# Weights behind the last v, one load for the gate, and ranks between two halves of the scores in a fused attention and top-1 expert kernel

## The chip, the cores and the metric

One core of a Trainium2 chip runs the whole kernel. The metric is the device time of one execution in microseconds (us), lower is better; the kernel before took 479.04 us (median of three runs, 478.44 to 480.1).

## The reference

Lightning attention (batch 4, 8 heads, 768 positions, head size 64, blocks of 64 with a decaying key-value state) gives a 3072 x 512 matrix `x`. Each row goes to the one expert of eight with the highest gate logit:

```python
logits = x @ w_gate                       # 512 x 8
expert_idx = np.argmax(logits, axis=1)
gate_w = softmax(logits)[row, expert_idx]
for e in range(8):
    xe = x[expert_idx == e]
    out[expert_idx == e] = gate_w * (np.maximum(xe @ w1[e], 0) @ w2[e])   # 512x1024, 1024x512
```

## The kernel before

**Attention.** The work is cut into six steps `n` of 128 positions and, in each, two pairs of batches `b` = 0 and 2; I write (n,b) for such a piece, and twelve of them follow each other. For one piece `enter` starts the loads of q, k and v of (n+1,b) on SP's queue (512 KB each, three buffers), turns q and k on TensorE (`turn_q`, `turn_k`, L207) and copies them on ScalarE. `score` (L242) makes the scores in two halves of heads `s`, and VectorE masks them with the decay into `mt` (L248, four per piece). `attend_states` (L267), `grow` (L293, `cp`) and `attend` (L276) give the output `op` and the new state. The main loop overlaps three pieces: it leaves the last one (`leave`, `rows`: TensorE turns the output back and multiplies by the gate in one go with `back`, tile `tx`, L320; ScalarE copies it and stores it to `xs` in device memory, L329), enters the next, and attends the current one.

**Routing.** When the four batches of a step have left, `choose` finds the expert of each row on VectorE (`oh`, one-hot) and adds the one-hots up batch by batch (`ohc`, L364). `put` (L375) then multiplies on TensorE: `before` (strictly upper triangular) by `oh`, and `ones` by the sums `ohc`; that is each row's rank among the rows of its expert. VectorE adds the expert's base and makes the address `slot_i` (L384 to L389), and GpSimd scatters the entries to `slots` in device memory (L391, two per piece). The first four steps fill the list of expert 0 early: when the entries of step 3 are stored, `start_early` loads `list_0a` on SP's queue (L416), gathers its 256 rows `xg` (L440) and runs them through expert 0 as pass 0a while the last rows of attention finish.

**Experts.** Passes 0a, 0b and experts 1 to 7 follow. `ph`, `po` and `p` are TensorE's matrix products there.

**What sets the order.** Instructions that are pinned (`pin`) keep the program's order on their engine; the others are placed by a scheduler. A wait on one of an engine's instructions holds all behind it. Loads that SP and ScalarE issue take completion semaphores in turn, and a load waits for the one that last used its semaphore. On-chip accumulators are eight banks: scores 0 to 3, `cp` 4, `rank` 5, `op` 6 and 7, `tx` 4 to 7. The last `tx` on banks 6 and 7 has to be copied out before the next `op` goes there.

Of the kernel before, what the change touches and what calls it, by code (L numbers as in the profile page):

```python
# [10 lines left out]
F32 = mybir.dt.float32  # L11
BF16 = mybir.dt.bfloat16
I32 = mybir.dt.int32
AX = mybir.AxisListType
# [7 lines left out]
def kernel(  # L22
# [29 lines left out]
    nc = tc.nc  # L52
    B, H, S, D = q.shape
# [112 lines left out]
    def pick(per_e, e):  # L166

        if isinstance(e, int):
            return per_e[e]
        return per_e[bass.ds(e, 1)].squeeze(0)  # L170

    def load_weights(e):
        w1t = wpool.tile([P, DC, F], F32, tag="w1", name="w1t")
        nc.sync.dma_start(out=w1t, in_=pick(w1_r, e))
        w2t = wpool.tile([P, FC, MD], F32, tag="w2", name="w2t")
        nc.sync.dma_start(out=w2t, in_=pick(w2_r, e))
        return w1t, w2t

    weights = []
# [9 lines left out]
    def bank(i, shape, name):  # L189
        return ps.tile(shape, F32, tag=f"bank{i}", name=name)  # L190
# [7 lines left out]
    def pin(inst):  # L198
        tc.keep_in_program_order(inst)
# [109 lines left out]
                    out=sd, in0=to, in1=sdec.unsqueeze(1).to_broadcast(shp), op=ALU.mult))  # L309
                nc.vector.tensor_add(to, m.cp, sd)  # L310

    def rows(m, b, lg):

        x = work.tile([P, MD], F32, tag="x", name="x", bufs=3)
        tx = [bank(4 + 2 * b + w, [P, HP // 2, 2, W], f"tx{w}") for w in range(2)]
        for hp in range(HP):
            c, j = hp // 2, hp % 2
            for w, t in ((0, 0), (1, 1), (0, 1), (1, 0)):
                flat = tx[w].rearrange("p c j w -> p c (j w)")
                pin(nc.tensor.matmul(  # L320
                    flat[halves[t], c, j * D:j * D + W],
                    lhsT=m.xT[b][halves[w], hp, halves[t]], rhs=back[halves[w], b, hp, :],
                    start=(hp == 0), stop=(hp == HP - 1), skip_group_check=True))
        to = x.rearrange("p (c j u e) -> p u c j e", c=HP // 2, j=2, u=2)
        for w, t in enumerate(tx):
            nc.scalar.copy(lg[:, w], t[:, :, 0, D:])
            nc.scalar.copy(to[:, w ^ b], t[:, :, :, :D])  # L327
        r0 = 1 + (m.n * B + m.b + b) * C
        nc.scalar.dma_start(out=xs[r0:r0 + C, :], in_=x)  # L329

    def choose(n, bs, lg):
        nb = len(bs)
        shp = [P, nb, E]
        parts, lg = lg, small.tile(shp, F32, tag="lg_sum", name="lg_sum")
        pin(nc.vector.reduce_sum(lg, parts.rearrange("p b w c e -> p b e (w c)"), axis=AX.X))
        mx = small.tile([P, nb, 1], F32, tag="mx", name="mx")
# [12 lines left out]

        more = 1 if (n, bs) == early else 0  # L350
        oh = small.tile([P, nb + more, E], BF16, tag=f"oh{more}", name="oh")
        if more:
            nc.gpsimd.memset(oh[:, nb], 0.0)
        nc.vector.tensor_tensor(out=oh[:, :nb], in0=key, in1=pick.to_broadcast(shp), op=ALU.is_equal)

        sm = small.tile([P, nb], F32, tag="sm", name="sm")
        nc.vector.reduce_sum(sm, ex, axis=AX.X)
        nc.vector.tensor_scalar_add(sm, sm, 1e-9)
        nc.vector.reciprocal(entry[:, n, bs[0]:bs[0] + nb, 2], sm)

        ohc = small.tile([P, nb + 1, E], BF16, tag="ohc", name="ohc")
        nc.vector.tensor_copy(ohc[:, 0], so_far[0])
        for i in range(nb):
            nc.vector.tensor_add(ohc[:, i + 1], ohc[:, i], oh[:, i])  # L364
        so_far[0] = ohc[:, nb]
        return n, bs, oh, ohc

    def put(n, bs, oh, ohc):


        nb = len(bs)
        shp = list(oh.shape)
        rank = bank(5, shp, "rank")
        for lhs, rhs in ((before, oh), (ones, ohc[:, :shp[1]])):
            mm = nc.tensor.matmul(rank, lhsT=lhs, rhs=rhs, start=(lhs is before),  # L375
                                  stop=(lhs is ones))

            if (n, bs[-1]) != (NSTEP - 1, B - 1):
                pin(mm)
        if shp[1] > nb:  # L380
            nc.vector.tensor_copy(had, rank[:, nb, 0:1])
        shp[1] = nb
        place = small.tile(shp, F32, tag="place", name="place")
        nc.vector.tensor_add(place, rank[:, :nb], base[0].unsqueeze(1).to_broadcast(shp))  # L384
        nc.vector.tensor_mul(place, place, oh[:, :nb])
        slot = small.tile([P, nb], F32, tag="slot", name="slot")
        nc.vector.reduce_sum(slot, place, axis=AX.X)
        slot_i = small.tile([P, nb], I32, tag="slot_i", name="slot_i")
        nc.vector.tensor_copy(slot_i, slot)  # L389
        def store(i):  # L390
            put = nc.gpsimd.indirect_dma_start(  # L391
                out=slots, out_offset=bass.IndirectOffsetOnAxis(ap=slot_i[:, i:i + 1], axis=0),
                in_=entry[:, n, bs[i], :], in_offset=None)

            tc.declare_no_dep(put.ins, group="put", reason="disjoint rows of the lists")
            tc.add_to_no_dep_group("put", put.ins)
            return put

        return store
# [254 lines left out]
    def enter(n, b):  # L654
        if n + 1 < NSTEP:
            loaded[n + 1, b] = load(n + 1, b)
        if (n, b) == (NSTEP - 2, B - 2):
            weights.append(load_weights(0))
        m = SimpleNamespace(n=n, b=b, qT=[], qsT=[], kT=[], kd=[], mt=[], xT=[])
        m.q, m.k, m.v = loaded[n, b]  # L660

        for s, turn_one in (((0, turn_q), (1, turn_q), (0, turn_k), (1, turn_k)) if not (n or b)
                            else ((0, turn_q), (0, turn_k), (1, turn_q), (1, turn_k))):
            turn_one(m, s)
        return m
# [19 lines left out]
    def give_places(group):  # L685

        waiting.append((group, put(*group), 0))

    def leave(m):
        for b in range(2):  # L690
            n, bs = group_of[m.n, m.b + b]
            i = bs.index(m.b + b)
            if i == 0:
                lgs[0] = small.tile([P, len(bs), 2, HP // 2, E], F32, tag="lg", name="lg")
            rows(m, b, lgs[0][:, i])
            if i == len(bs) - 1:

                pending.append((n, bs, lgs[0]))
# [25 lines left out]
    for s in range(2):  # L724
        score(cur, s)

    by_chunk = moe_w_gate.rearrange("(c j u d) e -> j u d c e", c=HP // 2, j=2, u=2)
    for j, u, b in itertools.product(range(2), range(2), range(2)):
        pin(nc.scalar.dma_start(
            out=back[halves[u ^ b], b, j::2, D - j * D:D - j * D + E], in_=by_chunk[j, u]))  # L730
    for i in range(len(order)):
        if last:
            leave(last)

        ahead = enter(*order[i + 1]) if 0 < i < len(order) - 1 else None
        attend_begin(cur)
        if cur.n < NSTEP - 1:
            attend_states(cur)
            decide()
# [12 lines left out]
        if i == 0:  # L752
            ahead = enter(*order[1])
        update(cur)
        if i == 0:
            later_decays()

        if chosen:
            give_places(chosen.pop())
        if ahead:  # L760
            store_places()
        if i == 1:
            empty_lists()
        if ahead and cur.n < NSTEP - 1:
            for s in range(2):
                score(ahead, s)
        last, cur = cur, ahead
    leave(last)
    decide()
    store_places(lambda inst: inst)  # L770
    give_places(chosen.pop())
    store_places(lambda inst: inst)


# [122 lines left out]
```

## Time and profile before

| | |
|---|---|
| median of three runs | 479.04 us |
| the profiled execution: its time, its span | 477.91 us, 476.1 us |
| TensorE matmul busy | 443.6 us (93%) |
| TensorE weight load busy | 367.0 us (77%) |
| VectorE, ScalarE, GpSimd busy | 243.7, 130.8, 252.9 us |
| moved by DMA | 72.71 MB, mean 153 GB/s |

The span is from the first to the last instruction; 1.8 us of the execution lie around it. Times in the rows are from the span's start. PE is TensorE's matmuls, PEld its weight loads, DVE VectorE, ACT ScalarE, POOL GpSimd, SP the engine that issues most loads; a q behind the name is the sequencer or queue of that engine. In brackets stands how long an engine was idle before an instruction and what ended the idle time. [...] TensorE's busy time is modelled, so a busy TensorE is not one at its peak.

### The profile page before, as it was taken

The page shows a single profiled execution, that of the slowest core. Times are in us where ns is not written, and L with a number is a line of the kernel's source. Part 1 is how long each engine was busy: PE and PEld are TensorE (multiplying, and loading weights), DVE is VectorE, ACT ScalarE, POOL GpSimd, SP SyncE. Part 2 cuts the span into 40 slices and gives each one's busy share as a digit, 9 for nine tenths or more (in the row PEclk, how much of TensorE's full clock was granted, in tenths as well). Part 3 has the DMA queues.
Part 4 walks back from the last instruction along what each step waited for, and adds up shares of the span by engine and source line. Part 5 has one row for each costly group of instructions (what it writes and reads, how often), then busy time and mean ns, then how long its engine had stood idle before and what let it go on. Part 6 is the DMA issues. An engine that isn't in the chain of part 4 may idle for free.

```text
span 476.1 us, 9780 instructions
## 1 busy us (share of the span) xinstructions
PE 443.6 (93%) x4023; PEld 367.0 (77%) x4023; DVE 243.7 (51%) x481; ACT 130.8 (27%) x327; POOL 252.9 (53%) x204
## 2 busy tenths in 40 slices
PE   4778988879789999999999999999999999999994
PEld 4667887869668484984996699599689779879863
DVE  3637475566634018475248534934843753564421
ACT  3334644443531022230123212212312311311210
POOL 6124445544243889985927663883793764531001
PEclk9979999999989999999999999999999999999998
DMA  9999999999723946735235360624426316001001
GB/s 178 177 233 256 240 207 236 222 296 260 171 87 97 375 121 201 245 100 173 86 136 176 91 220 1 234 79 174 178 83 222 124 73 222 1 18 46 1 19 51
DMA packets 100422, 72.71 MB, mean 153 GB/s; under 512 B 81811, under 2 KB 81815, under 8 KB 100368
## 3 DMA queue, kind: packets, MB, share of 16 engines
q1 hardware_dynamic: 90608, 52.49, 42.3%
q0 software_dynamic: 5008, 13.16, 8.7%
q10 hardware_dynamic: 4752, 6.33, 4.0%
q8 instruction: 34, 0.56, 0.5%
q14 instruction: 20, 0.16, 0.1%
HBM read 58.90 MB, written 13.16 MB: 151 GB/s over the span
## 4 chain that ended last, share of the span: by engine, by line
PE 70%; issue 3%; DMA 1%; POOL 1%; DVE 1%; POOLq 0%; ACT 0%
PE p L553 27%; PE p L581 18%; PE po L612 17%; PE ph L477 4%; PE tp L463 3%; DMA xg<-xs,list_0a 1%; POOL slots L391 0%; PE op L267 0%; PE tx L320 0%; POOLq L850 0%; DVE o L593 0%; PE rank L375 0%; DVE xgT L468 0%; POOL out_dram L446 0%; DVE hT L456 0%
## 5 line engine op out<-in xcount | busy, mean ns | idle before, releaser
L612 PE MATMUL po<-w2t,hT 128*128 128x512 f32 (+5 forms) x224 | 81.0, 596 | 0.0
L612 PEld LDWEIGHTS po<-w2t,hT 128*128 128x128 f32 (+5 forms) x224 | 30.5, 161 | 38.2 <-issue 37.9
L446 POOL DMA_INDIRECT out_dram<-o,list x24 | 23.7, 987 | 60.2 <-DVE o L618 31.6
L564 ACT ACTIVATE hT<-hT 128x408 f32<-128x408 f32 (+4 forms) x56 | 29.5, 527 | 90.5 <-DVE hT L562 90.5
L232 POOL TENSOR_TENSOR kd<-k_in,kdec 128x512 f32<-128x512 f32 x20 | 20.4, 1037 | 48.4 <-issue 22.2
L553 PE MATMUL p<-xgT,w1t 128*128 128x204 f32 (+4 forms) x224 | 41.5, 328 | 0.0
L553 PEld LDWEIGHTS p<-xgT,w1t 128*128 128x128 f32 x224 | 37.6, 190 | 1.2 <-issue 0.9
L517 POOL TENSOR_TENSOR t_q<-w2t 128x1024 f32<-128x1024 f32 x7 | 16.5, 2357 | 39.9 <-PE p L553 39.9
L391 POOL DMA_INDIRECT slots<-entry,slot_i x24 | 23.6, 981 | 23.2 <-DVE slot_i L389 15.5
L248 DVE TENSOR_TENSOR mt<-sp,decay 128x512 f32<-128x512 f32 x48 | 29.9, 682 | 10.5 <-PE sp L242 10.4
L593 DVE SCALAR_TENSOR_TENSOR o<-p,list,o 128x256 f32<-128x256 f32 x28 | 13.6, 484 | 32.9 <-PE p L581 17.0
L440 POOL DMA_INDIRECT xg<-xs,list x24 | 25.8, 1074 | 6.6 <-issue 5.0
L242 PEld LDWEIGHTS sp<-qT,kT 64*128 64x128 f32 x384 | 22.4, 188 | 7.4 <-ACT xT L285 4.2
L218 DVE TENSOR_TENSOR qsT<-tq,qdec 128x512 f32<-128x512 f32 x20 | 13.8, 692 | 26.3 <-ACT qT L214 26.3
L581 PE MATMUL p<-w2t,hT 128*128 128x256 f32 x112 | 26.8, 382 | 0.0
L581 PEld LDWEIGHTS p<-w2t,hT 128*128 128x128 f32 x112 | 21.0, 190 | 7.0 <-issue 4.5
L242 PE MATMUL sp<-qT,kT 64*128 64x128 f32 x384 | 24.8, 279 | 0.7 <-ACT kT L226 0.6
L517 POOL TENSOR_TENSOR t_v<-w2t 128x1024 f32<-128x1024 f32 x7 | 16.5, 2359 | 16.3 <-PE p L553 16.3
L276 PE MATMUL op<-mt,v_in 128*64 128x128 f32 x384 | 23.3, 273 | 1.2 <-ACT x L327 1.2
L207 PE MATMUL tq<-ident,q_in 128*128 128x128 f32 x96 | 16.9, 304 | 7.6 <-DMA q_in<-in_q_dram 7.6
L562 DVE TENSOR_TENSOR hT<-p,u_qsT 128x408 f32<-128x408 f32 (+4 forms) x28 | 15.7, 560 | 15.8 <-PE p L553 15.8
L477 PE MATMUL ph<-xgT,w1t 128*128 128x256 f32 (+1 forms) x128 | 23.0, 337 | 0.0
(159 smaller groups left out, 931.2 us busy)
## 6 DMA issues: line engine op xcount, KB each, us to landing
w1t<-in_moe_w_dram SPq DMA_DIRECT2D x8, 2048.0 KB, 7.9
w2t<-in_moe_w_dram SPq DMA_DIRECT2D x8, 2048.0 KB, 9.5
v_in<-in_v_dram SPq DMA_DIRECT2D x12, 512.0 KB, 8.7
xs<-x ACTq DMA_DIRECT2D x24, 256.0 KB, 5.9
q_in<-in_q_dram SPq DMA_DIRECT2D x11, 512.0 KB, 8.9
k_in<-in_k_dram SPq DMA_DIRECT2D x11, 512.0 KB, 8.3
q_in<-in_q_dram SPq DMA_DIRECT2D x2, 256.0 KB, 4.6
k_in<-in_k_dram SPq DMA_DIRECT2D x2, 256.0 KB, 5.3
```

The lines of the kernel that those rows point to most:

```text
L242: pin(nc.tensor.matmul(sp[u][:, i, b, :], lhsT=m.kT[s][halves[u], i, b, :], rhs=m.qT[s][halves[u], i, b, :], start=(i == 0 and b == 0), st ...
L248: nc.vector.tensor_mul(mt[:, u], sp[u], decay[:, u, s * HP // 2:(s + 1) * HP // 2].unsqueeze(2).to_broadcast(shp))
L276: pin(nc.tensor.matmul(out_at(m, b, u, hp), lhsT=m.v[:, b, 2 * hp + u, :], rhs=m.mt[hp // 2][:, u, hp % 2, b, :], start=(first and hp == 0 ...
L391: put = nc.gpsimd.indirect_dma_start(out=slots, out_offset=bass.IndirectOffsetOnAxis(ap=slot_i[:, i:i + 1], axis=0), in_=entry[:, n, bs[i] ...
L440: nc.gpsimd.indirect_dma_start(out=dst, out_offset=None, in_=xs[:rows, :], in_offset=bass.IndirectOffsetOnAxis(ap=idx, axis=0))
L446: put = nc.gpsimd.indirect_dma_start(out=out, out_offset=bass.IndirectOffsetOnAxis(ap=idx, axis=0), in_=src, in_offset=None, bounds_check= ...
L477: nc.tensor.matmul(ph, lhsT=w1t[:, dc, fc * P:(fc + 1) * P], rhs=m.xgT[:, dc, :], start=(dc == 0), stop=(dc == DC - 1))
L517: return nc.gpsimd.tensor_tensor(out=o, in0=x, in1=y, op=ALU.subtract)
L553: nc.tensor.matmul(p[:, i, :], lhsT=lhs[:, dc, (c + i) * P:(c + i + 1) * P], rhs=rhs[:, dc, :], start=(dc == 0), stop=(dc == DH - 1))
L564: nc.scalar.activation(outs[i][k], outs[i][k], ACT.Relu)
L581: nc.tensor.matmul(p, lhsT=lhs[:, fc, :], rhs=rhs[:, fc, :], start=(fc == 0), stop=(fc == FC // 2 - 1))
L612: nc.tensor.matmul(po[part], lhsT=m.hT[:, fc, t * P:t * P + w], rhs=w2t[:, fc, :], start=(i < k), stop=(i >= FC - k), skip_group_check=True)
```

## The change

The loads of expert 0's weights are pinned behind the load of the last v. The gate weights come in one load to a tile `gates`, from which GpSimd makes eight copies into `back`, in place of eight loads. The ranks of a step are made between the two halves of the scores; the sums over batches are made by TensorE (`ones` times the one-hots of the first i batches, added to the columns of the batches behind), and VectorE keeps only one running sum `so_far`. ScalarE copies the ranks out of the bank, and the first address operation is pinned behind the masks before it. The rows of the last piece but one use banks 2 and 3 in place of 6 and 7.

```diff
-    def load_weights(e):
+    def load_weights(e, pin=lambda inst: inst):
...
-        nc.sync.dma_start(out=w1t, in_=pick(w1_r, e))
+        pin(nc.sync.dma_start(out=w1t, in_=pick(w1_r, e)))
...
-        tx = [bank(4 + 2 * b + w, [P, HP // 2, 2, W], f"tx{w}") for w in range(2)]
+        tx = [bank(banks[b] + w, [P, HP // 2, 2, W], f"tx{w}") for w in range(2)]
...
+        new = small.tile([P, E], F32, tag="new", name="new")
+        nc.vector.reduce_sum(new, oh[:, :nb].rearrange("p b e -> p e b"), axis=AX.X)
+        old, so_far[0] = so_far[0], small.tile([P, E], BF16, tag="so_far", name="so_far", bufs=3)
+        nc.vector.tensor_add(so_far[0], old, new)
...
-        ohc = small.tile([P, nb + 1, E], BF16, tag="ohc", name="ohc")
-        nc.vector.tensor_copy(ohc[:, 0], so_far[0])
-        for i in range(nb):
-            nc.vector.tensor_add(ohc[:, i + 1], ohc[:, i], oh[:, i])
...
+    def ranks(n, bs, oh, old):
...
+        terms = [(rank, before, oh),
+                 (rank, ones, old.unsqueeze(1).to_broadcast(shp))]
+        terms += [(rank[:, all_b - i:], ones, oh[:, :i]) for i in range(last, 0, -1)]
...
+        got = small.tile(shp, F32, tag=f"rank{all_b - nb}", name="rank_in")
+        nc.scalar.copy(got, rank)
...
-            weights.append(load_weights(0))
+            weights.append(load_weights(0, pin))
...
-    for j, u, b in itertools.product(range(2), range(2), range(2)):
-        pin(nc.scalar.dma_start(
-            out=back[halves[u ^ b], b, j::2, D - j * D:D - j * D + E], in_=by_chunk[j, u]))
+    gates = const.tile([P, HP, E], F32, name="gates")
+    pin(nc.scalar.dma_start(out=gates, in_=moe_w_gate.rearrange("(c p) e -> p c e", p=P)))
+    for j, b, u in itertools.product(range(2), range(2), range(2)):
+        nc.gpsimd.tensor_copy(back[halves[u ^ b], b, j::2, D - j * D:D - j * D + E],
+                              gates[halves[u], j::2, :])
...
-            leave(last)
+            leave(last, (4, 6) if i < len(order) - 1 else (4, 2))
...
+        score_now = ahead and cur.n < NSTEP - 1
+        if score_now:
+            score(ahead, 0)
+        ranked = give_ranks()
+        if score_now:
+            score(ahead, 1)
+        for group in ranked:
+            give_places(group)
```

On SP's queue the loads of the last pieces stood in this order before (names with the number of their buffer: 1336 to 1338 are (4,2), 1548 to 1550 (5,0), 1725 to 1727 (5,2)):

```order
L93 DMA q_in_1548<-in_q_dram 128x16x64
L174 DMA w1t_1731<-in_moe_w1_dram 128x4x1024
L93 DMA v_in_1338<-in_v_dram 128x16x64
L93 DMA k_in_1549<-in_k_dram 128x16x64
L93 DMA q_in_1725<-in_q_dram 128x16x64
L93 DMA v_in_1550<-in_v_dram 128x16x64
L93 DMA k_in_1726<-in_k_dram 128x16x64
L176 DMA w2t_1733<-in_moe_w2_dram 128x8x512
L93 DMA v_in_1727<-in_v_dram 128x16x64
L416 DMA list_0a_2041<-slots_64 128x2x4
```

and now in this one (1344 to 1346 are (4,2), 1559 to 1561 (5,0), 1736 to 1738 (5,2)):

```order
L93 DMA q_in_1559<-in_q_dram 128x16x64
L93 DMA k_in_1560<-in_k_dram 128x16x64
L93 DMA v_in_1346<-in_v_dram 128x16x64
L93 DMA q_in_1736<-in_q_dram 128x16x64
L93 DMA k_in_1737<-in_k_dram 128x16x64
L93 DMA v_in_1561<-in_v_dram 128x16x64
L93 DMA v_in_1738<-in_v_dram 128x16x64
L174 DMA w1t_1742<-in_moe_w1_dram 128x4x1024
L176 DMA w2t_1744<-in_moe_w2_dram 128x8x512
L429 DMA list_0a_2082<-slots_64 128x2x4
```

Both weight loads have moved behind all loads of q, k and v, and both still stand ahead of `list_0a`.

On TensorE this stood at the first of four like places (steps 0 to 3), where `op` is the attention of one piece and `sp` the scores of the next, which go on for 14 more rows:

```order
L276 MATMUL op_601<-mt,v_in 64x128 x2
L375 LDWEIGHTS before
L375 MATMUL rank<-oh,before 128x32
L375 LDWEIGHTS ones
L375 MATMUL rank<-ohc,ones 128x32
L242 MATMUL sp_695<-qT,kT 128x128
L242 MATMUL sp_696<-qT,kT 128x128
```

and now, from the end of the first half of the scores (682, 683) to the second (703, 704):

```order
L242 MATMUL sp_683<-qT,kT 128x128
L378 LDWEIGHTS before
L378 MATMUL rank<-oh,before 128x32
L378 LDWEIGHTS ones
L378 MATMUL rank<-none_yet,ones 128x32
L378 LDWEIGHTS ones
L378 MATMUL rank<-oh,ones 128x24
L378 LDWEIGHTS ones
L378 MATMUL rank<-oh,ones 128x16
L378 LDWEIGHTS ones
L378 MATMUL rank<-oh,ones 128x8
L242 MATMUL sp_703<-qT,kT 128x128
```

Eight score matmuls now stand between the attention and the ranks, and the ranks are five matmuls, of which only `oh` is new from VectorE.

On VectorE, at the fourth place (step 3, whose entries fill `list_0a`), the addresses stood ahead of the masks:

```order
L362 COPY ohc<-ohc 128x8
L381 COPY had<-rank 128x1
L384 TENSOR_TENSOR place<-rank,ebase 128x32
L712 TENSOR_SCALAR skip<-had 128x1
L385 TENSOR_TENSOR place<-place,oh 128x32
L714 TENSOR_SCALAR skip<-skip 128x1
L387 TENSOR_REDUCE slot<-place 128x4
L717 TENSOR_TENSOR ebase_late<-ebase_late,skip 128x1
L389 CAST slot_i<-slot 128x4
L248 TENSOR_TENSOR mt<-sp_1868,decay 128x512
```

and now they stand among them:

```order
L248 TENSOR_TENSOR mt<-sp_1864,decay 128x512
L392 COPY had<-rank_in 128x1
L395 TENSOR_TENSOR place<-rank_in,ebase 128x32
L728 TENSOR_SCALAR skip<-had 128x1
L398 TENSOR_TENSOR place<-place,oh 128x32
L730 TENSOR_SCALAR skip<-skip 128x1
L400 TENSOR_REDUCE slot<-place 128x4
L733 TENSOR_TENSOR ebase_late<-ebase_late,skip 128x1
L248 TENSOR_TENSOR mt<-sp_1885,decay 128x512
L248 TENSOR_TENSOR mt<-sp_1886,decay 128x512
L402 CAST slot_i<-slot 128x4
```

The cast that GpSimd's scatter waits for has moved behind all four masks; ScalarE's copy `rank_in` lies between the ranks and `had`.

## Rows read from the trace of the kernel before

**Rows 1.** Chain that ended last: start us, us, what.

```profile
114.46 12.31 issue
...
128.86 5.53 DMA xg<-xs,list_0a
...
144.31 10.47 PE ph L477 x48
```

**Rows 2.** Seven stretches: busy time and instructions of each engine, PEclk, DMA share, GB/s.

```profile
10.00:14.00 4.00, 4.00 (x86) 3.88 (x88) 2.95 (x5) 0.39 (x1) 0.44 (x1) 1.00 1.40 216
14.00:18.00 4.00, 3.12 (x34) 2.50 (x32) 2.63 (x8) 2.40 (x6) 2.04 (x2) 1.00 0.48 75
23.00:30.00 7.00, 4.08 (x24) 3.41 (x26) 1.09 (x2) 1.92 (x4) 0.00 (x0) 0.51 1.07 237
30.00:115.00 85.00, 75.72 (x1716) 68.48 (x1714) 54.29 (x134) 38.53 (x117) 42.44 (x50) 1.00 1.09 239
115.00:125.00 10.00, 10.00 (x200) 9.29 (x198) 5.86 (x18) 4.91 (x15) 0.00 (x0) 1.00 1.11 308
135.00:139.00 4.00, 3.72 (x40) 2.90 (x41) 1.34 (x6) 1.67 (x4) 0.14 (x2) 0.58 0.01 1
145.00:469.00 324.00, 324.00 (x1614) 261.72 (x1612) 161.02 (x243) 70.07 (x147) 191.64 (x111) 1.00 0.38 128
```

**Rows 3.** Timeline from 7 to 28 us: start us, us, engine, line, what.

```profile
7.89 2.34 SPq L93 DMA_DIRECT2D k_in<-in_k_dram  x1
9.81 5.75 ACTq L729 DMA_DIRECT2D back<-in_moe_w_gate_dram  x8
15.70 0.37 SPq L93 DMA_DIRECT2D v_in<-in_v_dram  x1
23.13 1.09 PE L207 MATMUL tq<-ident,q_in 128*128 128x128 f32 x4 [2.12 <-DMA q_in<-in_q_dram]
27.00 1.09 PE L207 MATMUL tk<-ident,k_in 128*128 128x128 f32 x4 [2.79 <-DMA k_in<-in_k_dram]
```

**Rows 4.** Waits of SP's queue, whole run: who, whom for, us in total, times, longest.

```profile
SPq L416 <- DMA slots<-entry,slot_i: 8.7, 1, 8.7
SPq L93 <- DMA back<-in_moe_w_gate_dram: 5.4, 1, 5.4
```

**Rows 5.** Waits of PE's matmuls from 30 to 145 us.

```profile
PE rank L375 <- DVE ohc L364: 4.5, 4, 1.3
...
PE tp L463 <- DMA xg<-xs,list_0a: 1.6, 1, 1.6
PE op L276 <- ACT x L327: 1.2, 1, 1.2
PE rank L375 <- DVE oh L354: 1.2, 2, 1.1
```

**Rows 6.** Timeline at the fourth rank place, 105 to 109 us.

```profile
105.89 0.18 PE L375 MATMUL rank<-oh,before 128*128 128x40 bf16 x1 [0.15 <-DVE oh L354]
107.22 0.18 PE L375 MATMUL rank<-ohc,ones 128*128 128x40 bf16 x1 [1.15 <-DVE ohc L364]
107.33 2.06 PE L242 MATMUL sp<-qT,kT 64*128 64x128 f32 x32
107.44 0.16 DVE L381 COPY had<-rank 128x1 f32<-128x1 f32 x1
108.23 0.17 DVE L389 CAST slot_i<-slot 128x4 int32<-128x4 f32 x1
108.53 2.48 DVE L248 TENSOR_TENSOR mt<-sp,decay 128x512 f32<-128x512 f32 x4
```

**Rows 7.** Timeline of the chain to the early pass.

```profile
111.19 1.12 SPq L93 DMA_DIRECT2D v_in<-in_v_dram  x1
113.50 0.96 POOL L391 DMA_INDIRECT slots<-entry,slot_i  x1 [0.19 <-issue]
121.05 1.79 SPq L416 DMA_DIRECT2D list_0a<-slots  x1
134.44 0.55 PE L463 MATMUL tp<-ident,xg 128*128 128x128 f32 x3 [1.64 <-DMA xg<-xs,list_0a]
```

**Rows 8.** DMA issues, 112 to 114 and 148 to 150 us: KB each, us to landing.

```profile
v_in<-in_v_dram SPq DMA_DIRECT2D x1, 512.0 KB, 14.5
...
list_0b<-slots SPq DMA_DIRECT2D x1, 4.0 KB, 2.6
```

More of the change, by code (lines that the diff above doesn't have):

```diff
@@ L170, in pick @@
         return per_e[bass.ds(e, 1)].squeeze(0)
-    def load_weights(e):
+    def load_weights(e, pin=lambda inst: inst):
         w1t = wpool.tile([P, DC, F], F32, tag="w1", name="w1t")
-        nc.sync.dma_start(out=w1t, in_=pick(w1_r, e))
+        pin(nc.sync.dma_start(out=w1t, in_=pick(w1_r, e)))
         w2t = wpool.tile([P, FC, MD], F32, tag="w2", name="w2t")
-        nc.sync.dma_start(out=w2t, in_=pick(w2_r, e))
+        pin(nc.sync.dma_start(out=w2t, in_=pick(w2_r, e)))
         return w1t, w2t
@@ L310, in update, with rows @@
                 nc.vector.tensor_add(to, m.cp, sd)
-    def rows(m, b, lg):
+    def rows(m, b, lg, banks):
         x = work.tile([P, MD], F32, tag="x", name="x", bufs=3)
-        tx = [bank(4 + 2 * b + w, [P, HP // 2, 2, W], f"tx{w}") for w in range(2)]
+        tx = [bank(banks[b] + w, [P, HP // 2, 2, W], f"tx{w}") for w in range(2)]
         for hp in range(HP):
@@ L354, in choose, with put @@
         nc.vector.tensor_tensor(out=oh[:, :nb], in0=key, in1=pick.to_broadcast(shp), op=ALU.is_equal)
+        new = small.tile([P, E], F32, tag="new", name="new")
+        nc.vector.reduce_sum(new, oh[:, :nb].rearrange("p b e -> p e b"), axis=AX.X)
+        old, so_far[0] = so_far[0], small.tile([P, E], BF16, tag="so_far", name="so_far", bufs=3)
+        nc.vector.tensor_add(so_far[0], old, new)
         sm = small.tile([P, nb], F32, tag="sm", name="sm")
-        nc.vector.reduce_sum(sm, ex, axis=AX.X)
+        pin(nc.vector.reduce_sum(sm, ex, axis=AX.X))
         nc.vector.tensor_scalar_add(sm, sm, 1e-9)
         nc.vector.reciprocal(entry[:, n, bs[0]:bs[0] + nb, 2], sm)
-        ohc = small.tile([P, nb + 1, E], BF16, tag="ohc", name="ohc")
-        nc.vector.tensor_copy(ohc[:, 0], so_far[0])
-        for i in range(nb):
-            nc.vector.tensor_add(ohc[:, i + 1], ohc[:, i], oh[:, i])
-        so_far[0] = ohc[:, nb]
-        return n, bs, oh, ohc
-    def put(n, bs, oh, ohc):
+        return n, bs, oh, old
+    def ranks(n, bs, oh, old):
         nb = len(bs)
         shp = list(oh.shape)
+        all_b = shp[1]
         rank = bank(5, shp, "rank")
-        for lhs, rhs in ((before, oh), (ones, ohc[:, :shp[1]])):
-            mm = nc.tensor.matmul(rank, lhsT=lhs, rhs=rhs, start=(lhs is before),
-                                  stop=(lhs is ones))
+        last = all_b - 1
+        terms = [(rank, before, oh),
+                 (rank, ones, old.unsqueeze(1).to_broadcast(shp))]
+        terms += [(rank[:, all_b - i:], ones, oh[:, :i]) for i in range(last, 0, -1)]
+        for i, (to, lhs, rhs) in enumerate(terms):
+            mm = nc.tensor.matmul(to, lhsT=lhs, rhs=rhs, start=(i == 0),
+                                  stop=(i == len(terms) - 1), skip_group_check=True)
             if (n, bs[-1]) != (NSTEP - 1, B - 1):
                 pin(mm)
+        got = small.tile(shp, F32, tag=f"rank{all_b - nb}", name="rank_in")
+        nc.scalar.copy(got, rank)
+        return n, bs, oh, got
+    def put(n, bs, oh, rank):
+        nb = len(bs)
+        shp = list(oh.shape)
         if shp[1] > nb:
@@ L383, in put @@
         place = small.tile(shp, F32, tag="place", name="place")
-        nc.vector.tensor_add(place, rank[:, :nb], base[0].unsqueeze(1).to_broadcast(shp))
+        first = nc.vector.tensor_add(place, rank[:, :nb], base[0].unsqueeze(1).to_broadcast(shp))
+        if (n, bs[-1]) != (NSTEP - 1, B - 1):
+            pin(first)
         nc.vector.tensor_mul(place, place, oh[:, :nb])
@@ L687, in give_places, with give_ranks, leave @@
         waiting.append((group, put(*group), 0))
-    def leave(m):
+    def give_ranks():
+        return [ranks(*chosen.pop())] if chosen else []
+    def leave(m, banks=(4, 6)):
         for b in range(2):
@@ L694, in leave @@
                 lgs[0] = small.tile([P, len(bs), 2, HP // 2, E], F32, tag="lg", name="lg")
-            rows(m, b, lgs[0][:, i])
+            rows(m, b, lgs[0][:, i], banks)
             if i == len(bs) - 1:
@@ L725 @@
         score(cur, s)
-    by_chunk = moe_w_gate.rearrange("(c j u d) e -> j u d c e", c=HP // 2, j=2, u=2)
-    for j, u, b in itertools.product(range(2), range(2), range(2)):
-        pin(nc.scalar.dma_start(
-            out=back[halves[u ^ b], b, j::2, D - j * D:D - j * D + E], in_=by_chunk[j, u]))
+    gates = const.tile([P, HP, E], F32, name="gates")
[3 more added lines that the diff above has]
+                              gates[halves[u], j::2, :])
     for i in range(len(order)):
         if last:
-            leave(last)
+            leave(last, (4, 6) if i < len(order) - 1 else (4, 2))
         ahead = enter(*order[i + 1]) if 0 < i < len(order) - 1 else None
@@ L756 @@
             later_decays()
-        if chosen:
-            give_places(chosen.pop())
+        score_now = ahead and cur.n < NSTEP - 1
[6 more added lines that the diff above has]
+            give_places(group)
         if ahead:
@@ L763 @@
             empty_lists()
-        if ahead and cur.n < NSTEP - 1:
-            for s in range(2):
-                score(ahead, s)
         last, cur = cur, ahead
@@ L770 @@
     store_places(lambda inst: inst)
-    give_places(chosen.pop())
+    give_places(*give_ranks())
     store_places(lambda inst: inst)
```

## The prediction

> **What bounds the kernel now.** I read the chain of waits first. From 144.31 us it is TensorE's matmuls alone to the end, and before that it runs through one long wait (12.31 us up to 126.77) and the transfer of the early rows `xg` [rows 1]. The stretches say the same: from 145 to 469 us TensorE is busy 324.00 of 324.00 us [rows 2]. So behind 144 us nothing of this change can save or cost more than the matmuls it adds, and any time won ahead of it moves the end by as much. From 30 to 115 us TensorE is busy 75.72 of 85 us, so 9.3 us are open there [rows 2]. [...] Last, its waits from 30 us on: 4.5 us for `ohc` and 1.2 us for `oh` at the ranks, 1.2 us for a bank that ScalarE has not emptied, 1.6 us for `xg`; q, k and v are not among them [rows 5].
>
> **The change part by part.** The sum is made against the profiled execution, 477.91 us; the median of the runs is 479.04, so 1.1 us go on top at the end.
>
> *One load for the gate.* SP's load of v of (0,2) was issued only at 15.70 us, though SP was done with the load ahead of it at 7.89 + 2.34 = 10.23; it had waited 5.4 us for one of the eight gate loads [rows 3, 4], whose semaphore it takes over. In the changed program that load waits for the first half of the first q instead, long landed. The transfers show what the wait costs: 75 GB/s from 14 to 18 us after 216 from 10 to 14 [rows 2], that is 4 x (1 - 75/216) = 2.6 us of transfer not made. All loads behind come at least that much sooner. At most the two waits go, 4.9 us [rows 3]. I take 3.3: the 2.6, and some of the 1.1 us for which the first store of 256 KB (at 237 GB/s, [rows 2]) now comes behind k of (1,0) rather than into it. [...] The eight copies on GpSimd lie ahead of 19 us, where `back` is first used, and GpSimd waits there for k anyway. If they were late they would hold `tx` and the next kd by a us or two.
>
> *Ranks between the halves.* At the four places TensorE waits 4.5 + 1.2 = 5.7 us [rows 5]; the fourth shows how: 0.15 for `oh`, then 1.15 for the sums [rows 6]. The first half of the scores, 2.06/2 = 1.03 us, now covers the wait for `oh` (1.1 at its longest [rows 5]), and no sum is waited for. Added are three matmuls at three places and four at the fourth, 13 in all. One costs 107.33 - 107.22 = 0.11 us up to the next weight load [rows 6], so 1.4; at 0.18 and a weight load each it would be 3.6, hidden altogether nothing. Net 4.3, between 2.1 and 5.7. VectorE has fewer operations ahead of the masks; ScalarE's seven copies lie in its idle time.
>
> *The banks.* The 1.2 us for ScalarE's copies [rows 5] go, but they lie ahead of the wait for `xg` and count only if that no longer ends last.
>
> TensorE alone would thus come to the transposes of `xg` 3.3 + 4.3 + 1.2 = 8.8 us sooner: it waited from 134.44 - 1.64 = 132.8 [rows 7], now from 124.0.
>
> *The chain to `xg`.* At the fourth place TensorE is 3.3 + (5.7 - 1.3 - 9 x 0.11) = 6.7 us ahead. But the cast now stands behind all masks. Counted from the end of the attention (105.89 - 0.15, about 105.7), it ended at 108.40 [rows 6]; now: half the scores and a start of 0.2 to 106.9, four masks of 2.48 together, seven small operations of 108.23 - 107.44 = 0.8, the cast 0.17, so 110.4. That is 2.0 later, and the scatters are 4.7 sooner: the last at 108.8 instead of 113.50. Its landing released the list at 121.05, 7.5 us behind [rows 7], so now 116.3. On SP's queue behind the list's scatters wait only lists of later passes, which are far off. The weights: the last v is free to be loaded when the attention of (4,0) ends, 105.7 - 6.7 = 99.0; behind it come 0.5 MB of v, 4.2 MB of weights and 0.5 MB of stores; 5.2 MB at 308 GB/s [rows 2] are 17 us, plus 2 for the way, so 118. A list in a free queue took 2.6 us [rows 8], so it lands at 118.9, behind the weights. Before, the gathers were released at 126.77 [rows 1]: 7.9 sooner. If the list takes as long as before (5.7) it is 4.7; if TensorE ends last it is 8.8. I take 7.8.
>
> The trace on the order in the queue: the list, issued at 121.05 behind a v that was issued at 111.19 and landed 14.5 later at 125.7, let the gathers go at 126.77; the next list, with nothing ahead, took 2.6 us [rows 1, 7, 8]. [...]
>
> *The clock and the rest.* TensorE now waits 2.5 us for `xg` (124.0 to 126.6) in place of 1.64. After the old wait the clock was 0.58 from 135 to 139 us [rows 2], about 1.7 us lost. I add 0.3, between a gain of 1.7 and a loss of 1.7. [...] The last two groups add two matmuls, 0.2.
>
> Sum: -7.8 + 0.3 + 0.2 = -7.3. 477.91 - 7.3 + 1.1 = 471.7 us. Its own range, from the ends of the chain (4.7 and 8.8 sooner give 474.8 and 470.7) and a part of the clock's, is 469.5 to 475.
>
> **The rivals.**
>
> *The list waits out the weights.* If the 5.2 MB drain at the 239 GB/s of 30 to 115 us [rows 2] they take 21.8 + 2 us from 99.0, to 122.8, and the list lands at 123.4: 3.4 sooner than before, so 479.04 - 3.4 + 0.5 = 476.1. For it: the same queue, and the last v may wait for its buffer. Against: weights came in larger pieces at 308.
>
> *Transfers set the pace.* The DMA share is 1.09 from 30 to 115 us [rows 2]. If the loads can't come faster, the 5.7 us come back as waits for q, k and v, and only the start's 2.6 stays: 476.4. Against: no such wait among TensorE's now [rows 5], and 2.1 MB of weights leave that stretch.
>
> *TensorE ends last.* The list is ready by 124, as it would be if the scatters land faster: -8.8, and up to 2 for the clock: about 469.3. Against: 7.5 us for a scatter under load [rows 7].
>
> *Slower: the addresses behind the masks.* The chain to `xg` gets 2.0 us longer on VectorE. If TensorE is not ahead at the fourth place, since loads hold it, the list goes at 123, behind weights that began only at 105.7 and drain by 125; `xg` is 2 us later, the clock takes up to 1.7, the matmuls 0.2: about 482. It decides from the point at which TensorE's lead there is under 2.0 us. For it: the masks and the pinned first address operation leave no other order. Against: a lead of 3.4 from the three places before alone.
>
> *It doesn't do what it says.* The load of v meets another late semaphore, and the half scores don't cover `oh`: nothing is won, about 478.5.
>
> **How the numbers follow.** The forecast has 0.53, the list behind the weights 0.13, the pace of transfers 0.08, TensorE last 0.13, slower 0.08, nothing 0.05. I predict 471.7. The range goes from 467.8 (TensorE last, with the clock) to 477.2 (over both cases of a small gain) and leaves out the last two, some 0.15. A difference of 0.3%, 1.4 us, is what a measurement of this kernel can tell from none. Faster by more: 0.53 + 0.13 + 0.08 + 0.13 = 0.87; within: 0.05; slower: 0.08.
>
> **What would show it.** Right: the load of v of (0,2) issued near 10.3 us and no hole in the transfers behind 14; `tk` of (1,0) starting near 23.7; no wait over 0.3 us at the four rank places; the list issued near 116 and `xg` there near 126.6, with TensorE waiting 2 to 3 us for it; the chain unchanged behind, its 48 `ph` starting near 137. Wrong: waits for q, k or v on TensorE after 30 us (pace of transfers); the list more than 4 us from issue to the gathers, behind w2 (first rival); no wait at the transposes of `xg` (TensorE last); scatters of the fourth group later than 108.68 (slower).

## The result, and the profile after

The changed kernel took 473.48 us (median of four runs, 471.81 to 474.82) against 478.74 us for the one before beside it (476.71 to 480.1): a ratio of 0.9892, 95% interval 0.9842 to 0.9941, some 5.3 us. The prediction was 471.7, range 467.8 to 477.2. The profiled executions are closer, 474.09 against 477.91 us, so the traces have 3.8 us to explain.

The stretches of the changed kernel, columns as in [rows 2] (PEclk is TensorE's granted clock as a share of its full speed), with the steady end measured from 141 us:

```profile
14.00:18.00 4.00, 4.00 (x75) 3.82 (x74) 3.81 (x10) 1.12 (x3) 2.28 (x9) 1.00 1.37 214
23.00:30.00 7.00, 6.07 (x108) 5.76 (x108) 2.69 (x5) 3.93 (x10) 3.36 (x4) 1.00 1.23 281
30.00:115.00 85.00, 77.21 (x1683) 69.15 (x1681) 52.36 (x121) 39.10 (x120) 39.20 (x46) 0.98 1.02 240
115.00:125.00 10.00, 7.62 (x156) 6.87 (x154) 6.03 (x17) 3.79 (x13) 0.00 (x0) 1.00 0.78 247
135.00:139.00 4.00, 4.00 (x76) 3.15 (x75) 1.48 (x7) 1.94 (x10) 1.91 (x2) 1.00 0.15 51
...
141.00:465.00 324.00, 324.00 (x1614) 261.82 (x1612) 162.97 (x248) 70.08 (x147) 191.69 (x111) 1.00 0.38 128
```

The start is filled: 214 GB/s from 14 to 18 us where there were 75, and the clock is 1.00 from 23 to 30 us in place of 0.51. The last row has its 324.00 us of solid TensorE work 4 us sooner than [rows 2]. But between 115 and 125 us, where TensorE was busy all the time before, it now lacks 2.4 us.

The timeline of the changed kernel, as [rows 3, 6, 7] of before:

```profile
10.62 2.35 SPq L93 DMA_DIRECT2D v_in<-in_v_dram  x1
...
23.93 0.63 PE L207 MATMUL tk<-ident,k_in 128*128 128x128 f32 x4 [1.06 <-DMA k_in<-in_k_dram]
...
103.76 0.19 PE L378 MATMUL rank<-oh,before 128*128 128x40 bf16 x1
...
103.82 0.24 PE L378 MATMUL rank<-oh,ones 128*128 128x32 bf16 x4
...
104.67 0.50 SPq L176 DMA_DIRECT2D w2t<-in_moe_w_dram  x1
...
112.31 0.95 POOL L404 DMA_INDIRECT slots<-entry,slot_i  x1 [0.19 <-issue]
112.92 0.76 PE L276 MATMUL op<-mt,v_in 128*64 128x128 f32 x9 [1.27 <-issue]
119.61 0.37 SPq L429 DMA_DIRECT2D list_0a<-slots  x1
121.47 1.75 PE L276 MATMUL op<-mt,v_in 128*64 128x128 f32 x28 [2.38 <-issue]
126.02 0.99 POOL L453 DMA_INDIRECT xg<-xs,list_0a  x1 [12.76 <-DMA list_0a<-slots]
...
131.59 0.55 PE L476 MATMUL tp<-ident,xg 128*128 128x128 f32 x3 [0.69 <-DMA xg<-xs,list_0a]
```

The load of v went out at 10.62 instead of 15.70, and `tk` starts 3.1 us sooner. No wait stands ahead of the six rank matmuls, of which the last four begin 0.06 us behind the first. The list, though, was issued only 1.4 us sooner than before (119.61 against 121.05) and the gathers went 6.4 us behind it. What is new are idle times of TensorE with "issue" as their end, 1.27 and 2.38 us here: it waited for nothing that the profile can name. TensorE's waits from 30 to 145 us in the changed kernel (line of what waited, what it waited for, us in total, times, longest), to lay beside [rows 5]:

```profile
PE op L276 <- issue: 6.9, 4, 2.4
PE tx L320 <- issue: 2.3, 4, 0.9
PE cp L293 <- issue: 0.7, 2, 0.4
PE tp L476 <- DMA xg<-xs,list_0a: 0.7, 1, 0.7
...
PE rank L378 <- DVE oh L354: 0.4, 1, 0.4
...
PE op L267 <- issue: 0.3, 1, 0.3
```

The rank waits of 5.7 us and ScalarE's 1.2 us are gone. In their place stand 10.2 us of "issue" (6.9 + 2.3 + 0.7 + 0.3). Before, the same view has 2.9 us of it:

```profile
PE tx L320 <- issue: 2.6, 2, 1.6
...
PE op L267 <- issue: 0.3, 1, 0.3
```

These breaks come in step with the instructions, not with the work. The stretch between the first two of them (columns as above):

```profile
31.00:36.20 5.20, 4.88 (x126) 4.32 (x125) 2.58 (x6) 3.57 (x12) 0.39 (x1) 1.00 1.00 254
```

It holds about 126 matmuls and 126 weight loads, some 252 instructions on record. Counted with those of TensorE's sequencer (waits on semaphores, for example), the eleven breaks stand 256 records apart, or twice or three times 256, each within one record. The trace also has the transfers of instructions, as a DMA queue of its own (packets, MB, share of the engines' time; the changed kernel from 95 to 130 us):

```profile
q8 instruction: 6, 0.10, 1.2%
```

Its packets have 16,384 bytes, one to each step of 256, and each of the eleven breaks ends 1.3 to 1.7 us behind the landing of such a packet: the break up to 112.92 us behind one that landed at 111.48, the one up to 121.47 behind 119.88. So I read "issue" in these eleven breaks as TensorE waiting for its own instructions, block by block; the longest such break was 2.38 us.

The chain that ended last, in the changed kernel (as [rows 1]):

```profile
112.31 7.25 DMA slots<-entry,slot_i
119.61 5.41 DMA list_0a<-slots
...
127.32 4.23 DMA xg<-xs,list_0a
...
140.85 9.17 PE ph L490 x42
```

Scatter, list and gather follow each other without a gap, but TensorE waited only 0.69 us for their result: it came at 130.9 itself. The two chains end nearly together, so in this execution a gain on one alone would be capped by the other. That is what the experiments are about.

### The profile page after: what moved, and what is told of

It is laid out like the page before. It is cut to its first block, busy times and chain, and to the rows that moved or that the text cites. A ratio compares the mean times of both kernels' runs of the same rounds, so it can differ in the third digit from the quotient of the medians.

```text
span 472.3 us, 9797 instructions
## 1 busy us (share of the span) xinstructions
PE 445.8 (94%) x4041; PEld 368.9 (78%) x4041; DVE 244.5 (52%) x464; ACT 131.8 (28%) x334; POOL 255.0 (54%) x212
## 4 chain that ended last, share of the span: by engine, by line
PE 85%; DMA 5%; SPq 3%; issue 2%; DVE 1%; POOL 1%; ACT 0%; POOLq 0%; ACTq 0%
PE p L566 27%; PE p L594 18%; PE po L625 17%; PE ph L490 4%; PE sp L242 3%; PE op L276 3%; SPq L93 3%; PE tp L476 3%; PE tx L320 2%; PE cp L293 2%; PE op L267 2%; DMA k_in<-in_k_dram 2%; PE tq L207 2%; DMA slots<-entry,slot_i 2%; PE tk L207 2%
## 5 line engine op out<-in xcount | busy, mean ns | idle before, releaser
L276 PE MATMUL op<-mt,v_in 128*64 128x128 f32 x384 | 24.5, 274 | 6.9 <-issue 6.9
L242 PE MATMUL sp<-qT,kT 64*128 64x128 f32 x384 | 29.0, 304 | 0.0
L242 PEld LDWEIGHTS sp<-qT,kT 64*128 64x128 f32 x384 | 25.7, 208 | 2.4 <-issue 1.7
L276 PEld LDWEIGHTS op<-mt,v_in 128*64 128x64 f32 x384 | 21.3, 137 | 8.0 <-issue 7.9
## 6 DMA issues: line engine op xcount, KB each, us to landing
w2t<-in_moe_w_dram SPq DMA_DIRECT2D x8, 2048.0 KB, 20.2
```

The lines of the kernel that those rows point to most:

```text
L242: pin(nc.tensor.matmul(sp[u][:, i, b, :], lhsT=m.kT[s][halves[u], i, b, :], rhs=m.qT[s][halves[u], i, b, :], start=(i == 0 and b == 0), st ...
L276: pin(nc.tensor.matmul(out_at(m, b, u, hp), lhsT=m.v[:, b, 2 * hp + u, :], rhs=m.mt[hp // 2][:, u, hp % 2, b, :], start=(first and hp == 0 ...
```

## The experiments

The theories at the start. A: the list, behind the second weight load, sets the end; TensorE's own gains count up to that. B: the waits at the ranks had been covering the loading of TensorE's instructions, so that taking them away only uncovers it. Ratios are to the kernel before, run beside on the same chip, with a 95% interval; gains in us are differences of medians. Three chips were used, on which it took 477.88 us (e1 to e4), 488.55 (e5, e7 to e9) and 489.69 (e10 to e13).

**The gate load alone, on the kernel before (e1).**

```diff
-        pin(nc.scalar.dma_start(
-            out=back[halves[u ^ b], b, j::2, D - j * D:D - j * D + E], in_=by_chunk[j, u]))
...
+    pin(nc.scalar.dma_start(out=gates, in_=moe_w_gate.rearrange("(c p) e -> p c e", p=P)))
...
+        nc.gpsimd.tensor_copy(back[halves[u ^ b], b, j::2, D - j * D:D - j * D + E],
+                              gates[halves[u], j::2, :])
```

> Kernel before with the one gate load alone. Both theories: no hole in the transfers from 14 to 18 us, the attention of (0,2) starts 3 to 4.5 us sooner than 30.74. Theory A (a removed wait stays removed): the end moves by all of it, 474.5 to 476. Theory B (TensorE can't run ahead of the loads of its own instructions, 256 at a time, and the rank waits covered them): the rank waits are all still there, so the lead is kept as well, up to 1 us lost to new stalls that no semaphore explains: 475 to 477.

474.45 us, 0.9910 (0.9876 to 0.9944): 3.4 us from this part alone (4.3 by the ratio), where the whole change gave 5.3. In its trace a new wait stands among TensorE's:

```profile
PE op L267 <- ACT x L327: 3.3, 1, 3.3
```

ScalarE's copy of `x` was late there, so `op` could not have its bank. The chain of this trace shows what held it: the load of w1, from 84.72 to 97.84 us, then a store that ScalarE issues, then the copy. The changed kernel, whose weights no longer lie among those loads, does not show this wait.

**The change with the old ranks (e2).**

```diff
+        for i in range(nb):
+            nc.vector.tensor_add(ohc[:, i + 1], ohc[:, i], oh[:, i])
...
-        terms += [(rank[:, all_b - i:], ones, oh[:, :i]) for i in range(last, 0, -1)]
...
+        for lhs, rhs in ((before, oh), (ones, ohc[:, :shp[1]])):
...
-        ranked = give_ranks()
...
+        if chosen:
+            give_places(chosen.pop())
```

> Changed kernel with the ranks as they were before (in front of the scores, sums on VectorE); gate load, weights and banks as changed. A: the rank waits of 5.7 us return and TensorE is later by 4.3 at the last pieces; the list chain, whose masks no longer stand ahead of the addresses, by 1.4: 475 to 478. B: the rank waits return, but the 10.2 us of unexplained stalls (26 to 140 us) shrink by 4 to 6 us, so the time stays within 1.5 us of the changed kernel: 472 to 475.

474.88 us, 0.9929 (0.9894 to 0.9963): 0.4 points behind the whole change, with intervals that overlap: no difference is shown. Its waits of TensorE from 30 to 145 us:

```profile
PE rank L375 <- DVE oh L354: 3.1, 3, 1.5
PE rank L375 <- DVE ohc L364: 3.1, 4, 1.1
PE sp L242 <- issue: 2.3, 1, 2.3
PE tp L463 <- DMA xg<-xs,list_0a: 1.1, 1, 1.1
...
PE tx L320 <- issue: 0.5, 1, 0.5
```

6.2 us of rank waits are back, and "issue" is down from 10.2 to 2.8. This is what B expects. But it waits 1.1 us for `xg` as well, which is what A expects, so it does not part them.

**The change with the weights not pinned (e3).**

```diff
-            weights.append(load_weights(0, pin))
+            weights.append(load_weights(0))
```

> Changed kernel, the weight loads not pinned: w1 goes back ahead of the last two v, w2 ahead of the last one. A: the list has only the last v and part of w2 ahead of it, xg lands about as now; no change, 473 to 475. B: the same, but the unexplained stalls move from behind 103 us to 85 to 103, where w1 now runs; within 1 us of the changed kernel.

472.23 us, 0.9866 (0.9816 to 0.9916), no worse than the change. So putting the weights behind the last v was worth nothing by itself. Its list took 4.4 us from issue to landing and was issued at 116.86; `op L267` waited 3.4 us for ScalarE's `x`, as in e1 and again behind the load of w1 (82.88 to 95.49 us). The kernels with pinned weights do not show that wait.

**The change with both weight loads behind the first list (e4).**

```diff
-        if (n, b) == (NSTEP - 2, B - 2):
-            weights.append(load_weights(0, pin))
...
         m = make_pass(0, 0, EARLY, "0a")
+        weights.append(load_weights(0, pin))
         fetch(m, 1 + (NSTEP - 2) * B * C)
```

> Changed kernel, both weight loads behind the early list on SP's queue instead of ahead of it. A and B: the list takes 2.5 to 3.5 us from issue to landing instead of 6.4. A: the unexplained stalls of 1.3 and 2.4 us at 112 and 120 us stay, TensorE ends last as now, gain 0.7: about 473. B: these stalls are instruction loads held up by the weights' transfers; without those between 105 and 120 us they fall under 1 us together, and the end comes 2.5 to 4 us sooner: 469.5 to 471.

466.39 us, 0.9745 (0.9700 to 0.9789): the fastest, and clear of the change's own interval. The timeline of its list and weights:

```profile
111.17 0.37 SPq L429 DMA_DIRECT2D list_0a<-slots  x1
111.59 1.01 SPq L174 DMA_DIRECT2D w1t<-in_moe_w_dram  x1
112.65 0.50 SPq L176 DMA_DIRECT2D w2t<-in_moe_w_dram  x1
114.33 0.99 POOL L453 DMA_INDIRECT xg<-xs,list_0a  x1 [5.05 <-issue]
...
123.23 0.95 PE L476 MATMUL tp<-ident,xg 128*128 128x128 f32 x4
```

The last scatter started at 108.32 and the list could go 2.85 us later, against 7.3 in the change. The list took 2.2 us to landing, the gathers went at 114.33, and TensorE reached the transposes at 123.23 without a wait. The price is on the gathers, which now run beside the weights (issued at 111.59 and 112.65): 7.8 us to landing in this trace. They are still early. "Issue" adds up to 2.4 us here, in four breaks.

Both theories had this kernel slower, about 473 and 469.5 to 471, and the list alone does not account for it. In the change's profile TensorE waited 0.69 us for `xg`, so an earlier list could have saved little more there; in e4 it began the transposes 7.3 us sooner (123.23 against 130.57, the first of the four). Of these, 3.9 us stood already at the attention of (4,0), which began at 96.90 against 100.76: up to there the two programs do the same work, and e4 had fewer breaks and a clock of 1.00 from 30 to 96 us in place of 0.97. Behind it the change's breaks of 1.27 and 2.38 us, up to 112.92 and 121.47, are absent in e4. Those two steps of 256 instructions run while the change's weights are on their way (w1 issued at 103.20, w2 landed at 124.84). Over the profiles of this document (without e5): of the seven kernels with the weights ahead of the list, six have breaks of 1.8 to 3.7 us in these two steps and the kernel before has none; the six with the weights behind the list have none. (The view names ScalarE's copies `qT` or `kT` for three of these breaks, in e3, e7 and e9, of 1.28, 1.80 and 1.0 us; each stands ahead of the last 28 matmuls of an `op`, as the change's 2.38 does.) So that moving the weights let TensorE's instructions through is a rival to the list's place in the queue, and no experiment parts the two, since each moves the weights and the list past one another.

**The change once more, beside the next three (e9).** No edit.

> The changed kernel once more, for its time among the others and for a second profile. If its unexplained stalls (10.2 us from 26 to 140 us) come from the program alone they are the same within 1 us and at the same instructions; if they hang on how the transfers lie in a run, the places are the same and the sizes differ by some us. Time 472 to 475.

483.21 us, 0.9898 (0.9859 to 0.9937), as at first. Its waits of TensorE from 30 to 140 us:

```profile
PE cp L293 <- issue: 3.0, 8, 0.4
PE tx L320 <- issue: 2.4, 6, 0.4
...
PE op L276 <- issue: 1.5, 1, 1.5
PE op L276 <- ACT kT L226: 1.0, 1, 1.0
```

So which blocks come late is not a property of the program alone: of the six breaks of over 0.6 us in the first profile, the last two are left, with 1.5 us and with the 1.0 that the view puts down to `kT`. Instead there are many of 0.3 to 0.4, which every profile on the second and third chip has and which do not keep to the step of 256.

**Lighter transfers (e5).** q, k and v are read in pieces of 2 KB in another order, so that attention and routing work on other values; it is read up to 120 us only, and its total time (564.42 us) means nothing.

```diff
-                    out=t[:, b:b + per].rearrange("p b h d -> p (b h) d"),
+                    out=t[:, b:b + per].rearrange("p b h d -> p b (h d)"),
...
+                    in_=src[b0 + b:b0 + b + per].rearrange("b h s d -> b (h s d)")[
+                        :, n * C * H * D:(n + 1) * C * H * D].rearrange("b (p f) -> p b f", p=P))
```

> Changed kernel with q, k and v read in rows of 2 KB from consecutive memory, not in pieces of 256 B: the same bytes to the same tiles, but other values, so the routing is another and only the stretch up to 120 us is read. B (TensorE's instruction loads are held up by transfers): the same bytes take less of the DMA engines, and the unexplained stalls from 26 to 120 us fall from 8 to 10 us to under 3. A (they have nothing to do with the transfers): 8 to 10 us, as in the changed kernel.

From 26 to 120 us the DMA share fell from 0.99 (e9) to 0.72. TensorE's waits in that stretch:

```profile
PE cp L293 <- issue: 2.8, 8, 0.4
PE tx L320 <- issue: 2.3, 6, 0.4
```

The long break of e9 in that stretch is absent; the short ones stay, 5.1 us against 5.4. The attention of (0,2) started 4.2 us sooner than in e9 and that of (4,0) 4.1: in between, lighter transfers gained nothing. On this chip the short breaks thus did not go with the DMA share; for the long ones a single break decides nothing.

**The ranks alone, on the kernel before (e7).** The diff of e2, the other way.

> Kernel before with the ranks between the halves and their sums on TensorE, nothing else. A (a removed wait stays removed): the attention of (4,0), at 103.77 before, starts 3.4 us sooner, and the end comes 1.4 sooner by the list chain, 476.5. B (the rank waits covered TensorE's instruction loads): less than 2 us sooner at (4,0), unexplained stalls of 5 us or more in place of 2.9, and with the addresses 2.0 us later behind the masks the end is where it was or up to 1 us later: 477.5 to 479.

483.39 us, 0.9899 (0.9869 to 0.9929): 5.2 us. The attention of (4,0) began at 103.06, against 107.36 in e8 below, which ran on the same chip with the old ranks. B alone would have it near nothing; it falls as an explanation of the whole. The gates' eight loads and the old order of the weights are still there, and it gains about as much as the whole change.

**The weights behind the list alone, on the kernel before (e8).** The diff of e4.

> Kernel before with both weight loads behind the early list, nothing else. If the list waits out what stands ahead of it on SP's queue: list 2 to 3.5 us from issue to landing instead of 5.7, issued no later than 121, the 1.6 us wait for xg gone, then TensorE ends last: 475 to 476.5. If the order on that queue does not matter: 477 to 479.

488.86 us, 1.0011 (0.9989 to 1.0032): nothing. Two of its waits of TensorE from 26 to 145 us:

```profile
PE op L276 <- ACT lg L326: 3.7, 1, 3.7
PE rank L375 <- DVE oh L354: 3.4, 4, 1.1
```

The list is early here too, with the gathers at 126.00 and the transposes, without a wait, at 141.85: TensorE, with its old waits, ends last. But the wait of 3.7 us for `lg` stands in no other trace, and no row names what held ScalarE there; it may hide a gain of that size. So as measured neither the list alone helps (e8), nor do the parts together help more than one of them alone while the list stands behind the weights (e1, e7, e9).

**Part by part, with the list out of the way (e12, e10, e11, e13).** e12 is e4 again; e10 is e12 with the old ranks, e11 with the old gate loads, e13 with the old banks:

```diff
-            leave(last, (4, 6) if i < len(order) - 1 else (4, 2))
+            leave(last, (4, 6))
```

> The changed kernel with both weight loads behind the first list, once more, as the standard for the three kernels that run beside it. If the list's place in the queue is what held the change back: 0.972 to 0.979 of before, no wait of TensorE for the early rows. If the earlier run of it was luck in the instruction loads: about 0.989, as the changed kernel.

> The same with the old ranks (sums on VectorE, all scores behind the ranks). Theory A (with the list out of the way TensorE's own chain sets the end, so a part saves what its waits show): the 4.3 us of the ranks are lost, 0.9% slower than the kernel beside it, with 5 to 6 us of waits for oh and ohc. Theory B (part of those waits covered the loading of TensorE's instructions): 1.4 us lost, 0.3%, with fewer waits that no semaphore ends. Theory C (the list chain still ends last): no loss, and a wait for xg at the transposes.

> The same with the eight gate loads of before. Theory A: the 4.4 us by which the attention of (0,2) starts sooner with one load are lost, 0.9% slower than the kernel beside it, and the hole in the transfers from 14 to 18 us is back. Theory C: no loss, and a wait for xg at the transposes.

> The same with the last rows of the piece but one in banks 6 and 7 again. Theory A: the 1.2 us wait of op for ScalarE's copy is back and is lost, 0.25% slower than the kernel beside it. If ScalarE's copy in turn waits for a store held up by loads, 3 us and 0.7%. Theory C: no difference.

| kernel | us | ratio to before |
|---|---|---|
| e12, list first | 479.19 | 0.9788 (0.9749 to 0.9827) |
| e10, without the ranks | 487.09 | 0.9943 (0.9920 to 0.9965) |
| e11, without the gate load | 482.05 | 0.9843 (0.9812 to 0.9874) |
| e13, without the banks | 478.09 | 0.9767 (0.9732 to 0.9801) |

The ranks are worth 7.9 us here, the gate load 2.9 (its interval overlaps that of e12 a little), the banks nothing. On the ranks this is A, and more than the 4.3 that it named; inside the change, with the list behind the weights, no difference was shown (e2). TensorE's waits of e10 from 30 to 140 us:

```profile
PE tx L320 <- issue: 6.2, 16, 0.8
PE rank L375 <- DVE ohc L364: 2.8, 4, 1.1
PE rank L375 <- DVE oh L354: 2.7, 3, 1.1
PE tx L320 <- DVE place L384: 1.0, 1, 1.0
```

and of e12:

```profile
PE tp L476 <- DVE xgT L481: 3.8, 1, 3.8
PE tx L320 <- issue: 3.3, 9, 0.4
PE cp L293 <- issue: 2.8, 7, 0.4
```

5.5 us of rank waits and 1.0 for `place` stand in e10 alone; "issue" is much the same (7.7 against 6.1 us, most of it short breaks), and of breaks on the steps of 256 e10 has two and e12 none, where B wants fewer in e10: this speaks against B. The attention of (4,0) started at 105.87 in e10 and at 100.51 in e12, 5.4 apart, and the transposes at 138.53 and 127.56. In e12 TensorE then waited 3.8 us at their second half, where VectorE's copy `xgT` came late:

```profile
127.56 0.62 PE L476 MATMUL tp<-ident,xg 128*128 128x128 f32 x4
...
131.51 0.42 DVE L481 COPY xgT<-tp 128x256 f32<-128x256 f32 x1 [2.33 <-remote]
```

A late gather is not what the records show: two of the four transposes ahead of the copy are of the second gather's rows, and all four had run by 128.19; in e9, where the like wait was 1.8 us, both gathers had landed by 129.30, 4.3 us ahead of the transposes. VectorE's wait of 2.33 us ahead of the copy has only "remote" as its end in the view, and why the copy came so late stays open. In e13 `op` waited its 1.2 us for ScalarE's `x` again, and the wait for `xgT` was 1.3 instead of 3.8: the bank wait only moved.

e11 has 77 GB/s from 14 to 18 us and the clock at 0.76 from 23 to 30:

```profile
14.00:18.00 4.00, 3.90 (x58) 3.49 (x52) 3.95 (x8) 1.63 (x4) 2.21 (x2) 1.00 0.46 77
23.00:30.00 7.00, 5.38 (x64) 4.85 (x66) 2.08 (x3) 2.59 (x6) 1.62 (x2) 0.76 1.21 254
```

## Why the prediction was right, and where it was off

The direction, the range and the time (1.8 us off) held; two of the steps behind it did not, and that the time came so near is in part luck. In the profiled pair the wait for `xg` ended 2.9 us sooner (131.59 against 134.44) where the sum has 7.8, and the end came 3.8 sooner; the medians are 5.3 apart, and no row explains the 1.5 between.

**The start** came out as forecast or a little better: 3.3 forecast. `tk` starts 3.1 us sooner, and the clock from 23 to 30 us, for which the sum has no term, went from 0.51 to 1.00; the attention of (0,2) began 4.4 us sooner, at 26.35 against 30.74. e1 measured 3.4 (4.3 by the ratio), e11 2.9 us. The profile of before was the slowest start of all: with the one load (0,2) began at 26.0 to 27.7 in nine profiles, with the eight at 27.7 to 30.7 in four, and the clock from 23 to 30 us was 0.76 or 1.00 in either group but for that 0.51.

**The ranks.** 5.7 us of waits became 0.4, as forecast. The added matmuls, put at 0.11 us each, cost next to nothing: at the fourth place the last four of six begin 0.06 us behind the first, and the scores go on 0.24 us behind it, at 104.00. Forecast 4.3 net; 5.2 in e7, 7.9 in e10 against e12, and nothing clear of noise inside the change (e2). That was right in kind; the size depends on what stands beside it.

**"TensorE alone would thus come to the transposes 8.8 us sooner"** failed in the profiled execution. With the terms as measured (4.4, 5.3 of waits, 1.2 of banks) it should have been 10.9; it came at 131.59 - 0.69 = 130.9 instead of 132.8, 1.9 sooner. "Issue" grew by 10.2 - 2.9 = 7.3 us, and the clock's 0.98 from 30 to 115 us is up to 1.7 more; together the 9.0 that are missing. No step of mine had a price for the loading of TensorE's instructions, though the trace of before had it: its three breaks end 1.3 to 1.5 us behind instruction packets too. In e4, the same work up to that place with fewer breaks, the lead at (4,0) was 6.9 us, close to the forecast 6.7. The bank of e13 shows how the same happens with named waits.

**The list.** Forecast: issued 116.3, landed 2.6 us later, gathers 7.8 sooner. Measured: issued at 119.61, since the lead at the fourth place was 3.0 us (attention of (4,0) at 100.76 against 103.77) and not 6.7; 5.41 us until it was there, since w2, issued at 104.67, landed 20.2 us later at 124.84, just ahead of it; gathers released at 125.02 instead of 126.77, 1.8 sooner. Here the first rival was right: the list waited out the weights. I had the weights drained at 118, with 2 us for the way that no run shows; w2 landed 6.8 us later. The scatter's 7.25 us was as forecast (7.5). That the change gains with the weights behind the list is shown twice, by e4 and e12 (0.9745 and 0.9788 against 0.9892 and 0.9898); how much of this came by the list and how much by the missing breaks is not shown.

**The clock** behind the wait for `xg`: forecast 0.3 lost, a term that no run shows; it was 1.00 from 135 to 139 us instead of 0.58, after a wait of 0.69 us in place of 1.64. As an estimate, the 3.8 at the end less the 2.9 at the transposes leave about a microsecond for it.

**The banks** "count only if that no longer ends last": they did not count in e13, where the wait behind them took up the 1.2 us.

Of the other rivals: transfers did not set the pace, since no wait for q, k or v stands behind 30 us in the change's profile; TensorE did not end last alone, though it was 0.7 us from it; the addresses behind the masks cost 1.8 us, about the 2.0 counted (from the end of the attention of (4,0) to the end of the cast it was 4.5 us, before 2.7). The range's lower end, 467.8, is 0.6 below what its terms give (479.04 - 8.8 + 0.2 - 2 = 468.4); nothing hangs on it.

**Open** stays why a block of instructions lands late in one execution and not in another: there were six long breaks in the first profile (1.17, 0.66, 0.86, 2.08, 1.27 and 2.38 us), two in the second, and none to two in the five of the change with the list first. Open is also what the short breaks on the other two chips are, and how much of the difference between the profiles' 3.8 us and the runs' 5.3 the late blocks make.

## What to carry to other kernels

Before summing gains on one engine, look for the second chain that ends at the same wait, and price both; parts that are worth 1% each alone may give no more than 1% together (e1, e7 and e9). Where a small load starts a dependent chain, try the bulk loads of its queue behind it: two lines moved gave this change 1.1 to 1.5 points more (e12, e4), though nothing without it (e8), and such a move also changes what else the bulk loads run beside. An idle time that no semaphore ends can take the place of a wait that was removed (in the change's profile 6.5 us of waits at the ranks and for the bank went and 7.3 us of "issue" came), so give it a term in the sum.

## What the runs showed of the hardware

TensorE's idle times without a named cause went with the transfers of its instructions: in the profiles of before and of the change they were 14 breaks of 0.26 to 2.38 us between 26 and 145 us, all on steps of 256 recorded instructions and all ending 1.3 to 1.7 us behind the landing of a 16 KB packet of the instruction queue; e1 to e4 have 12 more, of 0.44 to 2.32 us. They made 10.2 us in the change's profile, 2.9 in that of before and 1.8 to 4.1 in e1 to e4. On two other chips most were of 0.3 to 0.4 us in `tx` and `cp`, stayed when the DMA share fell from 0.99 to 0.72, and the same kernel before was 2% slower there (488.55 and 489.69 us against 477.88).

The scatters' landing went with what ran beside them: 7.25 us with two weight loads under way, 2.8 us in e4 with those loads not yet issued. From the last scatter to the issue of the list it was 6.0 to 8.1 us in the seven kernels with weights ahead of the list and 2.4 to 4.5 in the six with the weights behind it. A list of 4 KB took 2.2 us in e4 with the weights behind it, and 5.41 us behind w2.
